# A two-level product kernel on one core: where weight sums, one PSUM add and the next x are placed

## The chip, the cores and the metric

The kernel runs on one core of a Trainium2 chip. The core has five engines that run side by side: TensorE (PE in the profile, its weight loads are PEld), VectorE (DVE), ScalarE (ACT), GpSimd (POOL) and SyncE (SP), which here only issues transfers. The metric is the time of one execution on the device, in microseconds (us), as the median of seven executions.

## The reference

The reference is an attention without softmax, followed by a feed-forward block that multiplies two projections of the same input:

```python
kv = np.einsum('bhsd,bhse->bhde', k, v)          # 8 batches, 8 heads, 576 tokens, 64 per head
out = np.einsum('bhsd,bhde->bhse', q, kv)
rms = np.sqrt(np.mean(out * out, axis=-1, keepdims=True) + 1e-06)
x = out / rms * g_norm                            # then (8,8,576,64) -> (4608, 512)
a = x @ w1                                        # 512 -> 1024
b = x @ w2
h = a * b @ w3                                    # 1024 -> 1024
return h @ w_out                                  # 1024 -> 512
```

All inputs to the kernel's arithmetic are 32-bit floats on the chip; the weights come in 64 bits and are converted first.

## The kernel before, in words

**Start.** The kernel converts the weights and multiplies `w3 @ w_out` into one matrix, `w3o_sb`, so that the feed-forward block becomes `(x@w1 * x@w2) @ w3o`. This ends near 84 us.

**Groups.** The tokens are worked in nine groups of 512. Groups T = 0 to 7 hold the first 512 tokens of one batch each; group T = 8 (called `B` in the code) holds the last 64 tokens of all eight batches. The order is 0 to 6, then 8, then 7 (L976). For every group there are two stages: the gates (`a * b`, kept in `ab`) and the projection (`ab @ w3o`).

**Products in the manner of Strassen and Winograd.** Each large product is cut into 2 x 2 blocks and made with seven products of blocks in place of eight (`winograd`, L611). This needs sums of the blocks of the weights (`sums`: s1, s2, s4, and s3 in the place of a21) and of the moving side (`combine`: t1, t2, t4, and t3 in the place of b12). The results are put together from the products in PSUM and from copies that ACT makes of some of them: p1, p5, u2 and u3. The copies u2 and u3 share one buffer, so u3's copy waits until u2 has been read.

**Gates (L743).** For T = 0 to 6 the gates go through p = 0 to 3, one scheme of seven products for each p; each gives one part of `ab` as four blocks c12, c22, c11, c21 (an add on DVE, L757, and a multiplication, L758; for c21 a copy on ACT and a multiplication, L753 and L754). After each p DVE sums the blocks of `ab` for the projection (`sum_ab`, L730). In the middle of each scheme stands `between`, which is called twice for each p and carries the attention of the next batch in pieces (`steps`, L519): k-v products, the q part, the norm (L378: squares on ACT, reduction L385 on DVE, square root L389 on ACT, reciprocal and multiplication on DVE) and the turning of x and q by copies on POOL (L291, L293, L305) and transposing transfers on SP (L295).

**Projection (`project_twice`, L1016).** From T = 1 on each of its seven block products is itself cut in the same way (two levels). DVE makes the inner sums (`sum_inner`, L1001, written into three rotating places `inner_sums[n % 3]`), PE makes seven times seven small products, ACT copies results from PSUM, and DVE joins them (`add`, L1089, and `finish`, L1066). The weights of this product are prepared once in T = 1, stored in DRAM, and loaded back for each projection (`load_b`, L979). The argument `ahead` is the list of four subtractions on DVE that combine the next group's x (`combine_x`); they were called after `sum_inner(2)`.

**The last two groups (T = 8 and T = 7, `TWICE`).** Their gates for p = 2 are made in the usual way, then those for p = 0 and 1 in two levels (`gates_of_two`, L824), then p = 3 in the usual way. The inner sums of the weights for these (7 sets of s1, s2, s4, called the weights' sums here) are made ahead by `prepare_w` (L770) in T = 3 and T = 4, stored to DRAM by three transfers for each set, and loaded back later (`load_w`). Each set takes three DVE instructions (L775 to L777), which go into one of the three places of `inner_sums`; before the change the sets took turns between the first and the third place.

In `gates_of_two` the products 0 and 2, 4, 6 go through one pair of PSUM banks (r1), 3 and 5 through another (r2), product 1 through a third (r3). p1 and p5, u2, u3 and a last one are copied to SBUF by ACT (`keep`); `add` on DVE adds a product to a copy straight from PSUM; `finish` joins the four parts.

**What sets the order.** PE, POOL and SP run their instructions in the order in which the program is written; so does DVE from p = 3 of a group to the end of its projection, and from `gates_of_two` to the end in the last two groups (`manual_schedule`). The other instructions of DVE, and ACT's, are put in order by a planner when the program is built: it may set an instruction earlier than where it is written, also among those whose order is written out. `tc.issue_after(ins)` keeps the instructions made inside it behind `ins` on the same engine; it says nothing of how far behind. On each engine an instruction that waits holds up all those behind it.

Of the kernel before, what the change touches and what calls it, by code (L numbers as in the profile page):

```python
# [3 lines left out]

# [8 lines left out]
FP32 = mybir.dt.float32  # L13
# [9 lines left out]
def kernel(  # L23
# [32 lines left out]
    nc = tc.nc  # L56
# [551 lines left out]
    def late_tile(name):  # L608
        return late_pool.tile([P, 7, P], FP32, name=name[0] if name[0] == "u" else name)
# [160 lines left out]
    def prepare_w():  # L770

        for n, (name, _) in enumerate(PRODUCTS):
            a11, a12, a21, a22 = w_blocks(name)
            s1, s2, s4 = inner_sums[2 * (n % 2)]
            nc.vector.tensor_add(s1, a21, a22)  # L775
            nc.vector.tensor_sub(s2, s1, a11)
            nc.vector.tensor_sub(s4, a12, s2)  # L777
            for i, s in enumerate((s1, s2, s4)):
                at = (3 * n + i) * 2 * P
                nc.sync.dma_start(  # L780
                    out=w_l2[:, at:at + 2 * P].rearrange("p (w m) -> p w m", w=2), in_=s
                )
            yield
# [40 lines left out]
    def gates_of_two(T):  # L824

        if not places:
            other = work.tile([P, 2, 2, NP // 2, N], FP32, name="xT")
            other = other.rearrange("p i j r n -> p (i j r n)")
            places.extend([other[:, 0:PART // 2], other[:, 1024:1024 + PART // 2]])
            other = work.tile([P, 2, 2, 4, D], FP32, name="xn", bufs=1)  # L830
            places.append(other.rearrange("p i l m d -> p (i l m d)")[:, 0:PART // 2])
            places[:] = [t.rearrange("p (n t) -> p n t", t=P) for t in places]

        def products(n, w, ps, new):
            a_name, b_name = PRODUCTS[n]
            a11, a12, s3, a22 = (t[:, w] for t in w_blocks(a_name))
            s1, s2, s4 = (
                loaded_w[q // 7][:, q % 7 * 2 * P + w * P:q % 7 * 2 * P + (w + 1) * P]
                for q in range(3 * n, 3 * n + 3)
            )  # L840
            b11, _, b21, b22 = (
                xb[T][b_name][:, c, i * P:(i + 1) * P] for c in range(2) for i in range(2)
            )
            t1, t2, t3, t4 = x_sums[n]
            seen = set()
            for place, x, y in (
                (0, a11, b11), (3, a12, b21), (1, a22, t4), (2, s1, t1), (6, s2, t2), (5, s4, b22),
                (4, s3, t3),
            ):
                nc.tensor.matmul(  # L850
                    ps[place // 4][:, place % 4, :], lhsT=x, rhs=y,
                    start=new and place // 4 not in seen, stop=True, skip_group_check=True,
                )
                seen.add(place // 4)
            if w == 1 and n in (2, 4, 6):
                load_b()
            return ps

        def banks(pool, tag):
            return [bank(pool, tag).rearrange("p (i n) -> p i n", n=P) for _ in range(2)]  # L860

        def keep(t, ps):
            nc.scalar.copy(t[:, 0:4], ps[0])
            nc.scalar.copy(t[:, 4:7], ps[1][:, 0:3])
            return t

        def add(z, ps):
            nc.vector.tensor_add(z[:, 0:4], ps[0], z[:, 0:4])
            nc.vector.tensor_add(z[:, 4:7], ps[1][:, 0:3], z[:, 4:7])

        def finish(z, w, i, j):

            def wide(i):
                return z[:, i:i + 1].to_broadcast([P, 2, P])

            dst = ab[i][:, 0:2, j, :].rearrange("p m (n t) -> p m n t", t=P)
            to = dst
            if w:
                to = late_pool.tile([P, 2, N], FP32, name="c").rearrange("p m (n t) -> p m n t", t=P)
            nc.vector.tensor_add(z[:, 6], z[:, 6], z[:, 0])  # L880
            nc.vector.tensor_add(z[:, 4:6], z[:, 4:6], wide(6))
            nc.vector.tensor_add(to[:, 1], z[:, 1:3], wide(4))
            nc.vector.tensor_add(to[:, 0], z[:, 3:6:2], z[:, 0:3:2])
            if w:
                nc.vector.tensor_mul(dst, dst, to)

        for w in range(2):
            r1 = products(0, w, banks(ps_mm, "mm"), True)
            p1 = keep(late_tile("p1"), r1)
            r3 = products(1, w, banks(ps_at, "at"), True)  # L890
            add(p1, r3)
            finish(p1, w, 0, 0)
            products(2, w, r1, False)
            z = keep(late_tile("u2"), r1)
            r2 = products(3, w, banks(ps_mm, "mm"), True)
            p5 = keep(places[2] if w else late_tile("p5"), r2)
            products(4, w, r1, False)
            u3 = keep(places[0], r1)
            nc.vector.tensor_add(p5, p5, u3)
            finish(p5, w, 1, 1)  # L900
            products(5, w, r2, False)
            add(z, r2)
            finish(z, w, 0, 1)
            products(6, w, r1, False)
            finish(keep(places[1], r1), w, 1, 0)
        loaded_w.clear()

    def sum_ab_two():
# [92 lines left out]
    def sum_inner(n, between=lambda: None, place=None):  # L1001

        s1, s2, s4 = ab_sums
        x = [ab[0][:, :, 0], s1, s2, s4, ab[0][:, :, 1], ab[1][:, :, 0], ab[1][:, :, 1]][n]
        a11, a12, a21, a22 = (
            x[:, 2 * j:2 * j + 2, i * P:(i + 1) * P] for i in range(2) for j in range(2)
        )
        s1, s2, s4 = inner_sums[(n if place is None else place) % 3]
        nc.vector.tensor_add(s1, a21, a22)  # L1009
        nc.vector.tensor_sub(s2, s1, a11)  # L1010
        nc.vector.tensor_sub(s4, a12, s2)
        between()
        nc.vector.tensor_sub(a21, a11, a21)  # L1013
        inner[n] = [a11, a12, a22, s1, s2, s4, a21]

    def project_twice(T, last, ahead, load_after):  # L1016
# [97 lines left out]
        p1 = keep("p1", r1)  # L1114
        load_b()
        sum_inner(2)
        for f in ahead:
            f()
        r2 = products(1)
        p5 = keep("p5", r2)  # L1120
        load_b()
# [2 lines left out]
        z = keep("u2", r1)  # L1124
        load_b()
        sum_inner(4)
        products(3, r2)
        if not done[T]:
            load_b()
# [136 lines left out]
    for n, T in enumerate(groups):  # L1266
        pieces = steps(T + 1) if n + 2 < NG else iter([])

        at = count()

        def between():
            next(pieces, lambda: None)()
            if T == 1:
                for _ in range(2):
                    if next(preparing, 0) == 0 and len(loaded_b) < 3:
                        load_b()
            if T in (3, 4) and next(at) in (0, 2, 3, 5):
                next(preparing_w, 0)
            if T == B - 2 and p == 2 and not replaced:
                replaced.append(True)  # L1280
                replace_a21()
# [11 lines left out]
        for p in range(NF):  # L1293
            if T in TWICE and p + 1 < NF:
                continue
            if T and p + 1 == NF:
                sum_1, sum_2, sum_4, sum_3 = sum_ab(p)
                following = {
                    "c12": [], "c22": [sum_1],
                    "c11": [  # L1300
                        lambda: sum_inner(0, lambda: all_of(f() for f in (sum_2, sum_3))),
                        lambda: sum_inner(1),
                    ],
                    "c21": [sum_4],
                }

                if T in TWICE:
                    following["c12"] += of_two[:1]
                    following["c22"] += of_two[1:]
                else:  # L1310
                    in_order = tc.manual_schedule(engines={mybir.EngineType.DVE})
                    in_order.__enter__()
                gates(T, p, between, lambda name: all_of(f() for f in following[name]))
                continue
            gates(T, p, between if T or p else lambda: None)
            if T == 0:
                if p + 1 < NF:
                    run(sum_w(p + 1))
                for n in range(2):
                    if len(converted) < len(todo):  # L1320
                        ahead = [copies["xT"] if p == 0 else copies["u3"][0], copies["u2"][p]][n]
                        with tc.issue_after(ahead.ins):
                            begin_next()
                        end_next()
                if p + 1 == NF:
                    allocate_projection()
                    run(*(f(i) for i in range(NF) for f in (sum_ab, combine_w3o)))
            else:
                run(sum_ab(p))
        last = n + 1 == NG  # L1330
        if T:
            project_twice(
# [40 lines left out]
```

## Time and profile before

| | |
|---|---|
| median of 7 executions | 765.32 us (765.01 to 766.04) |
| profiled execution, its own time | 765.32 us |
| its span, first to last instruction | 763.5 us |
| instructions | 15003 |
| granted TensorE clock, mean | 1.00 |
| transfers | 140.84 MB, mean 184 GB/s |
| stages in the span | start to 84 us; T=0 and 1 to 243; T=2 to 319; T=3 to 395; T=4 to 473; T=5 to 548; T=6 to 623; T=8 to 691; T=7 to the end |

How to read the lines: in the timeline each line gives the start in us from the span's start, the duration, the engine, the line of the kernel, the operation, what it writes and reads (by the program's names, buffer numbers left out), the shape and a count; in brackets stands how long the engine was idle just before and whose work ended that. Tiles cut from one larger buffer carry that buffer's name: `raw` holds, among others, the sums of `ab`, the first place of `inner_sums` and the output blocks; the third place is `inner_sums`; the second lies in the tail of `w3o_sb` and in `raw`. Ends of matmuls are modelled. The chain of work follows the span back from its end, at each step to what released it.

### The profile page before, as it was taken

Reading aid. Unit: us, or ns where it says so; the run is one execution under the profiler, and the core shown is the slowest. Engines: PE = TensorE matmul, PEld = TensorE weight load, DVE = VectorE, ACT = ScalarE, POOL = GpSimd, SP = SyncE. Lnnn points to the kernel's source line nnn. Section 1 sums busy time; section 2 is a strip of 40 time slices with the busy share of each in tenths; the row PEclk is TensorE's granted clock in tenths of the full one; section 3 lists DMA queues with packets and bytes.
Section 4 is the critical chain, followed back from the end, with each engine's and each line's share of the span. In section 5 each row is a group of like instructions: output and inputs, shape, how many; then the busy total and the mean of one; then the engine's idle time right before and its main releaser. Section 6 shows DMA issues by size and latency. Waiting matters only on the chain.

```text
span 763.5 us, 15003 instructions
## 1 busy us (share of the span) xinstructions
PE 755.1 (99%) x5943; PEld 661.0 (87%) x5943; DVE 585.7 (77%) x1167; ACT 263.4 (34%) x499; POOL 165.0 (22%) x190
## 2 busy tenths in 40 slices
PE   8999999999999999999999999999999999999998
PEld 6455788888899889988998899889988999999997
DVE  7978999548878568967786588567867777997797
ACT  6777763213322332232222322332233213322421
POOL 0000000223510442043104320431053125006100
PEclk9999999999999999999999999999999999999999
DMA  9997641338997835694669466835652470466244
GB/s 317 342 334 204 195 146 35 84 84 255 332 297 260 241 98 163 217 242 142 187 209 258 135 166 223 218 95 164 227 128 59 152 220 35 145 204 190 92 138 144
DMA packets 137050, 140.84 MB, mean 184 GB/s; under 512 B 77076, under 2 KB 124308, under 8 KB 136980
## 3 DMA queue, kind: packets, MB, share of 16 engines
q1 hardware_dynamic: 134528, 125.46, 55.0%
q10 hardware_dynamic: 2452, 14.42, 5.6%
q8 instruction: 47, 0.77, 0.4%
q14 instruction: 23, 0.19, 0.1%
HBM read 105.78 MB, written 19.14 MB: 164 GB/s over the span
## 4 chain that ended last, share of the span: by engine, by line
PE 83%; issue 6%; DMA 4%; DVE 3%; POOL 2%; ACT 1%; SPq 1%; POOLq 0%; ACTq 0%
PE mm L618 45%; PE mm L1051 19%; PE mm L597 7%; PE mm L850 5%; PE at L333 2%; PE at L416 2%; DMA raw<-in_moe_w_out_dram 1%; PE at L850 1%; PE at L584 1%; DMA w_l<-raw 1%; DMA xn<-xT 1%; DMA q_sb<-qT 1%; POOL xT L305 1%; POOL qT L305 1%; PE at L352 1%
## 5 line engine op out<-in xcount | busy, mean ns | idle before, releaser
L618 PE MATMUL mm<-xT,w_sb 128*128 128x256 f32 x720 | 165.2, 379 | 0.0
L618 PEld LDWEIGHTS mm<-xT,w_sb 128*128 128x128 f32 x720 | 136.3, 190 | 18.7 <-issue 0.5
L618 PE MATMUL mm<-xc,ws 128*128 128x256 f32 x512 | 116.3, 380 | 0.8 <-ACT p L631 0.8
L618 PEld LDWEIGHTS mm<-xc,ws 128*128 128x128 f32 x512 | 96.9, 190 | 14.9 <-ACT p L631 1.7
L631 ACT COPY u<-mm 128x512 f32<-128x512 f32 x66 | 38.7, 587 | 122.6 <-PE mm L618 114.0
L291 POOL COPY xT<-xn 128x1024 uint16<-128x1024 uint16 x26 | 31.1, 1226 | 179.4 <-DVE xn L394 179.4
L757 DVE TENSOR_TENSOR c<-mm,u 128x512 f32<-128x512 f32 x32 | 22.0, 688 | 59.7 <-PE mm L618 59.7
L631 ACT COPY p<-mm 128x512 f32<-128x512 f32 x66 | 38.5, 585 | 73.7 <-PE mm L618 66.0
L597 PE MATMUL mm<-chunks,ab 128*128 128x512 f32 x128 | 60.3, 603 | 1.7 <-DVE chunks L171 1.4
L618 PE MATMUL mm<-xc,w_sb 128*128 128x256 f32 x256 | 61.4, 383 | 0.0
L618 PE MATMUL mm<-xT,ws 128*128 128x256 f32 x240 | 57.3, 382 | 0.0
L758 DVE TENSOR_TENSOR ab<-c 128x256 f32<-128x256 f32 x96 | 52.7, 549 | 2.5
L618 PEld LDWEIGHTS mm<-xc,w_sb 128*128 128x128 f32 x256 | 47.8, 190 | 6.9 <-ACT u L631 0.3
L385 DVE TENSOR_REDUCE inv<-sq 128x8 f32<-128x512 f32 (+1 forms) x40 | 23.4, 626 | 35.4 <-ACT sq L384 35.4
L618 PEld LDWEIGHTS mm<-xT,ws 128*128 128x128 f32 x240 | 44.9, 190 | 6.2
L1051 PE MATMUL mm<-w3o_sb,ab 128*128 128x128 f32 x368 | 49.1, 276 | 0.2
L1051 PE MATMUL mm<-w3o_sb,raw 128*128 128x128 f32 x372 | 48.6, 276 | 0.0
L1051 PEld LDWEIGHTS mm<-w3o_sb,ab 128*128 128x128 f32 x368 | 45.5, 192 | 1.2 <-DVE ab L1013 0.6
L1051 PEld LDWEIGHTS mm<-w3o_sb,raw 128*128 128x128 f32 x372 | 44.9, 192 | 0.5 <-DVE raw L1009 0.2
L1062 ACT COPY u<-mm 128x512 f32<-128x512 f32 x23 | 13.5, 587 | 85.8 <-DVE raw L1075 57.1
L597 PEld LDWEIGHTS mm<-chunks,ab 128*128 128x128 f32 x128 | 21.8, 190 | 24.2 <-issue 15.8
L305 POOL COPY xT<-xn 128x1024 uint16<-128x1024 uint16 x26 | 30.7, 1208 | 50.9 <-DMA xn<-xT 50.9
(300 smaller groups left out, 1368.2 us busy)
## 6 DMA issues: line engine op xcount, KB each, us to landing
w3o_sb<-w3o_l SPq DMA_DIRECT2D x18, 896.0 KB, 4.8
raw<-in_moe_w_dram SPq DMA_DIRECT2D x31, 512.0 KB, 7.5
raw<-w3o_l SPq DMA_DIRECT2D x15, 896.0 KB, 4.6
w3o_sb<-w3o_l ACTq DMA_DIRECT2D x14, 896.0 KB, 4.5
k_sb<-in_k_dram SPq DMA_DIRECT2D x32, 256.0 KB, 4.2
v_sb<-in_v_dram SPq DMA_DIRECT2D x32, 256.0 KB, 4.7
q_sb<-in_q_dram SPq DMA_DIRECT2D x32, 256.0 KB, 4.7
out_dram<-raw SPq DMA_DIRECT2D x14, 512.0 KB, 3.6
```

Source lines behind the costliest of these rows:

```text
L291: nc.gpsimd.tensor_copy(to, src.rearrange("p a n w -> p w a n"))
L305: nc.gpsimd.tensor_copy(words(dst), src)
L333: nc.tensor.matmul(kv_ps[e * D:(e + 1) * D, r - rs[0], :], lhsT=k_sb[:, e, cols] if j < J else kl[:, 2 * r + e, :], rhs=v_sb[:, e, cols] i ...
L385: nc.vector.tensor_reduce(out=inv[:, i], in_=sq.rearrange("p (h d) -> p h d", d=D), axis=AX.X, op=ALU.add)
L416: nc.tensor.matmul(o_ps[l][tokens, n * D:(n + 1) * D], lhsT=qT[r][rows, e, i, tokens], rhs=kv_b[rows, e, r, :], start=True, stop=True,)
L597: nc.tensor.matmul(sums_ps[half][m], lhsT=w3T[half, c][:, m, :], rhs=chunks[:, c, 1, :], start=(c == 0), stop=(c == KF - 1),)
L618: nc.tensor.matmul(ps[:, u, :], lhsT=lhsT(a_name, u, c), rhs=rhs(b_name, c),  start=(u == 0 and c == 0 and to is None), stop=(c == chunks ...
L631: copies.setdefault(name, []).append(nc.scalar.copy(t, ps))
L757: nc.vector.tensor_add(c, one, two)
L758: nc.vector.tensor_mul(dst, c[:, 0, :], c[:, 1, :])
L850: nc.tensor.matmul(ps[place // 4][:, place % 4, :], lhsT=x, rhs=y, start=new and place // 4 not in seen, stop=True, skip_group_check=True,)
L1051: nc.tensor.matmul(to[:, i, :], lhsT=x[:, c, :], rhs=y[:, c, :], start=new and place // 4 not in seen, stop=(c == 1), skip_group_check=True,)
```

## The change

Three things move, and a few instructions go.

1. **Weights' sums.** They are no longer called inside `between`. In T = 3 and T = 4 they are called after `sum_ab(p)` and tied behind its last instruction: two sets after p = 1 and two after p = 2 in T = 3, two after p = 1 and one after p = 2 in T = 4. They now take turns through all three places of `inner_sums`. Their transfers on SP move with them in the written order.
2. **Third joined product of `gates_of_two`.** The product that was copied as u3 and then added to p5 is added to p5 straight from PSUM by `add`: two ACT copies and one DVE add of 896 elements become two DVE adds of 512 and 384. The buffers `places` shrink from three to two.
3. **Next x.** In `project_twice` the list `ahead` runs after `sum_inner(4)`, no longer after `sum_inner(2)`.

```diff
         for n, (name, _) in enumerate(PRODUCTS):
             a11, a12, a21, a22 = w_blocks(name)
-            s1, s2, s4 = inner_sums[2 * (n % 2)]
+            s1, s2, s4 = inner_sums[n % 3]
...
-            other = work.tile([P, 2, 2, 4, D], FP32, name="xn", bufs=1)
-            places.append(other.rearrange("p i l m d -> p (i l m d)")[:, 0:PART // 2])
...
-            p5 = keep(places[2] if w else late_tile("p5"), r2)
+            p5 = keep(places[1] if w else late_tile("p5"), r2)
             products(4, w, r1, False)
-            u3 = keep(places[0], r1)
-            nc.vector.tensor_add(p5, p5, u3)
+            add(p5, r1)
             finish(p5, w, 1, 1)
             products(5, w, r2, False)
             add(z, r2)
             finish(z, w, 0, 1)
             products(6, w, r1, False)
-            finish(keep(places[1], r1), w, 1, 0)
+            finish(keep(places[0], r1), w, 1, 0)
...
         sum_inner(2)
-        for f in ahead:
-            f()
         r2 = products(1)
...
         sum_inner(4)
+        for f in ahead:
+            f()
         products(3, r2)
...
-        at = count()
-
         def between():
...
-            if T in (3, 4) and next(at) in (0, 2, 3, 5):
-                next(preparing_w, 0)
...
             else:
-                run(sum_ab(p))
+                ops = [step() for step in sum_ab(p)]
+                with tc.issue_after(ops[-1].ins):
+                    for _ in range({(3, 1): 2, (3, 2): 2, (4, 1): 2, (4, 2): 1}.get((T, p), 0)):
+                        next(preparing_w)
```

More of the change, by code (lines that the diff above doesn't have):

```diff
@@ L1 @@
 from contextlib import ExitStack
-from itertools import count, islice
+from itertools import islice
 from types import SimpleNamespace
```

## The prediction

> **What bounds the kernel now.** I read the page first, then PE's pauses in the timeline, then what ended each. Groups of tokens are named by their T. Page, busy time and the chain's shares:
>
> ```profile
> PE 755.1 (99%) x5943; PEld 661.0 (87%) x5943; DVE 585.7 (77%) x1167; ACT 263.4 (34%) x499; POOL 165.0 (22%) x190
> PE 83%; issue 6%; DMA 4%; DVE 3%; POOL 2%; ACT 1%; SPq 1%; POOLq 0%; ACTq 0%
> ```
>
> PE is the bound and the change touches no matmul, so only PE's pauses can be won. In the timeline, weight loads start every 0.216 us in the gates (8 in 1.73) and every 0.112 in the inner products. A later start I count as a pause. From 84 us on, those of 0.15 us or more that are not in every group are: T=1's projection 0.26, 0.30, 0.15 (at 226, 231, 232); start of T=3 0.23 (322); T=4 0.24 (398) and 1.20 (413); T=6 0.29 and 0.25; T=8 0.17 and 0.38 (669, 671); T=7 0.19 and 0.38. Sum 4.0 us: no change of the other engines wins more. Two kinds matter. First, T=4, timeline of weight loads and of DVE and ACT:
>
> ```profile
> 408.24 0.84 DVE L775 TENSOR_TENSOR raw<-w_sb 128x256 f32<-128x256 f32 x1 [0.97 <-DMA w_l<-raw]
> 411.35 0.41 DVE L776 TENSOR_TENSOR raw<-raw,w_sb 128x256 f32<-128x256 f32 x1
> 411.79 0.43 DVE L777 TENSOR_TENSOR raw<-w_sb,raw 128x256 f32<-128x256 f32 x1
> 412.14 1.27 DVE L385 TENSOR_REDUCE inv<-sq 128x8 f32<-128x512 f32 x2
> 413.44 0.31 ACT L389 ACTIVATE inv<-inv,eps_col 128x16 f32<-128x16 f32 x1 [3.03 <-DVE inv L385]
> 413.66 1.05 ACT L631 COPY p<-mm 128x512 f32<-128x512 f32 x2
> 414.27 1.59 PEld L618 LDWEIGHTS mm<-xc,ws 128*128 128x128 f32 x8 [1.23 <-ACT p L631]
> ```
>
> A weight sum (L775) waits 0.97 us for the landing of an earlier sum's transfer; behind it on DVE stand two sums of ab, the other two weight sums and the norm's reduction; ACT stands at the square root that needs the reduction, with p1's copy behind it; and PE needs that copy to reuse the bank. Loads were due at 411.35 + 1.73 = 413.07 and came at 414.27. At the starts of T=3 and T=4 the same sums sit inside the tail of the projection before:
>
> ```profile
> 319.91 0.41 DVE L775 TENSOR_TENSOR raw<-w_sb 128x256 f32<-128x256 f32 x1
> ...
> 321.78 0.41 DVE L1075 TENSOR_TENSOR raw<-p 128x256 f32<-128x256 f32 x1
> ...
> 322.29 0.59 ACT L631 COPY p<-mm 128x512 f32<-128x512 f32 x1 [2.16 <-DVE raw L1075]
> 322.92 1.16 PEld L618 LDWEIGHTS mm<-xc,ws 128*128 128x128 f32 x6 [0.26 <-ACT p L631]
> ```
>
> The second kind is DVE as the chain itself, in T=8 (T=7 alike):
>
> ```profile
> 665.48 0.59 ACT L631 COPY u<-mm 128x512 f32<-128x512 f32 x1 [2.87 <-PE mm L618]
> 666.14 0.68 DVE L757 TENSOR_TENSOR c<-p,u 128x512 f32<-128x512 f32 x1
> 667.67 0.69 DVE L915 TENSOR_TENSOR raw<-ab,raw 128x512 f32<-128x512 f32 x1
> 671.85 0.52 PEld L1051 LDWEIGHTS mm<-w3o_sb,ab 128*128 128x128 f32 x4 [0.30 <-DVE ab L1013]
> ```
>
> **The change, part by part. A: the weights' sums.** The edge behind the last sum of ab keeps the seven sets (21 DVE sums of some 0.42 us, 21 transfers on SP) out of the projections' tails and out of T=4's first half. It moves them; none goes.
> What is taken away: in each tail six sums at a pitch of 0.33 to 0.45 us, 2.0 to 2.7 us; p1's copy then waits for PE alone, and the 0.23 and 0.24 go whole. In T=4 the wait (0.97), the first sum (0.76 until the next starts at 409.00) and the other two (0.79) leave the reduction 2.5 us earlier, 409.6 in place of 412.1. The square root then ends by 411.2, before p1's product is ready (first loads 411.35 + 0.2), and 1.20 goes whole. Were only the wait taken away, 0.97 of it would go. T=5 and T=6, which have no weight sums, start with no pause. Gain 0.23 + 0.24 + 1.20 = 1.67.
> What is added: two sets behind p = 1 in T=3 (from 348.6) and T=4 (from 424.6), two behind p = 2 in T=3 (from 365.0), one in T=4 (from 444.2). Alone, a set takes 3 x 0.45; beside POOL's copies single sums took 1.14 to 1.26 (at 333.7 and 350.3). Two sets are thus 2.0 to 4.5 us. The cover is DVE's idle time there, rows of DVE's timeline in T=3:
>
> ```profile
> 354.79 1.28 DVE L385 TENSOR_REDUCE inv<-sq 128x8 f32<-128x512 f32 x2 [2.79 <-ACT sq L384]
> ...
> 364.54 0.43 DVE L672 TENSOR_TENSOR raw<-ab,raw 128x256 f32<-128x256 f32 x1
> 368.22 0.69 DVE L757 TENSOR_TENSOR c<-mm,u 128x512 f32<-128x512 f32 x1 [3.25 <-PE mm L618]
> ...
> 373.20 0.42 DVE L1009 TENSOR_TENSOR raw<-ab 128x256 f32<-128x256 f32 x1
> ```
>
> After p = 1 there are 6.1 us in T=3 (348.6 to 354.8) and 6.8 in T=4 (the reduction at 431.45 waited 6.81): covered. After p = 2 in T=4 1.5 us for 1.35: covered. After p = 2 in T=3 3.25 us for 2.0 to 4.5, with POOL copying from 365.46 to 367.71: two sums at 1.2 and four at 0.45 are 4.2, so L757 starts about 0.9 late. Behind it, u3's copy (369.88 in the trace, after PE) needs L757 done: 368.22 + 0.9 + 0.69 = 369.8, just in time. If that cover is short, the projection's sums behind it start late, and they have only 0.15 us to spare (L1013 ends 375.55, PE loads its result at 375.70). Bounds of this cost: 0, and 4.5 - 3.25 = 1.3. I take 0.0, since 0.9 lies inside the slack.
> The transfers: SP is kept at the six DMAs until their sums are done, near 353.5, and the loads of k and v that followed at 352.35 come 1.2 us later; pair for pair they are read by PE in the next group, tens of us on. Cost 0. At 369 nothing follows on SP but L993 at 371.60, which waits for PE. The fourth set now uses the first buffer, which the projection's first sum (373.20) overwrites: its transfer, issued about 368.7, lands 1.8 to 2.0 us later in the quiet rows (347.80, 366.59), at 370.7; with the worst row (6.08, at 402.13) at 374.8, a wait of 1.6. I take the quiet rows, since SP's neighbours there are the same; 0, other end 1.6.
>
> **B: p5 + u3 straight from PSUM** (four times). ACT loses two copies (0.59 and 0.48), DVE's add of 896 elements (pitch 1.13, 654.28 to 655.41) becomes two from PSUM (pitch 0.60 + 0.58 = 1.18, L1090 and L1091 at 243.02 and 243.62). They start when the copy started (653.10), not at 654.28, so DVE's chain runs 1.1 us ahead. PE's seventh product in that bank must now wait for DVE: adds end at 654.3, loads are due at 654.97, 0.65 to spare (643.3 against 644.03 for w = 0). Where does the 1.1 go? DVE reaches c12's add at 663.8 (u2's copy at 662.03 + 1.74, as in T=3), not 664.48, and then c22's add, which needs u3's copy: 665.48 + 0.59 = 666.07, on PE's clock. It starts at 666.10 in place of 666.14. What is late next is ACT's copy, and L915's 0.6 behind it still stands. So 0.04 in each of T=8 and T=7, 0.08. Bounds: 0, and all of both groups' pauses, 1.12.
> At this place a rule speaks against the change: the Trainium skill, "Perfetto Trace Analysis", section "Optimizing Scalar/DVE Operations", puts a DVE instruction's access at about 60 ns on SBUF and 125 ns on PSUM, so two PSUM reads for one SBUF read are an estimated 0.19 us more DVE time each, 0.76 over four. By the rows above it is 0.05 each, 0.2 over four; by either the sum keeps its sign.
>
> **C: next x combined later.** Its four subtractions (0.79 + 0.61 + 0.60 + 0.60 = 2.6 us) pass behind sums 3 and 4, and all of it still ends where the add of u2 begins (385.50 in T=3), so DVE's later work does not move; SP, POOL and ACT have nothing in the step. Sums 3 and 4 come 2.6 us earlier. That takes away T=1's 0.30 and 0.15, where sum 3 ran at 231.27 while PE was at its product. But in T=1 DVE is busy without idle time to p1's last sum (245.33 to 245.75), and T=2's p1 copy waits for it (1.97 <-DVE raw L1075) and ends at 246.42; PE needed it at 243.07 + 3.35 = 246.42. PE arrives 0.45 earlier and waits 0.45 there. Gain 0, bounds 0 and 0.45.
>
> **Sum.** 1.67 + 0.08 + 0 = 1.75 us. The profiled execution took 765.32 us, a span of 763.5 and 1.8 around it, and equals the median of the seven runs, so 765.32 - 1.75 = 763.6 us. About 0.2%, 1.53 us, is what can be told from no change: below 763.8 counts as faster, above 766.85 as slower.
>
> **Rivals.**
> 1. T=3's second place has too little cover: DVE's lateness or the buffer's landing reaches the projection, 0.7 to 1.6 us are given back, 764.3 to 765.2. For it: 4.2 us of sums in 3.25 of idle time. Against: the quiet landings and u3's slack.
> 2. T=4's long pause is POOL's, not the sums': two sums of ab took 1.25 beside POOL's copy at 407.76 (rows L672). If the reduction stays behind them, half of 1.20 remains: 764.2 to 764.7. Against: the reduction could then start at 410.6 and still be in time.
> 3. Better: DVE's lead in B or C reaches PE, up to 1.04 and 0.45 more, 762.1 to 763.1. Against: u3's copy and p1's wait.
> 4. Slower: the edge sets only the earliest place of the sums, not the latest. If the order made for DVE puts the three sets of p = 2 into the projections, which have 0.15 us to spare, each costs 3 x 0.45 = 1.35 us of PE: 4.05, and 763.6 + 4.05 = 767.6. It decides from 1.75 + 1.53 = 3.3 us, that is from all three sets on; one set only eats most of the gain. For it: before, the sums did land inside projections. Against: DVE's idle time stands right behind the edge.
>
> **How the numbers follow.** Main case 0.56, 763.2 to 764.1, of which 0.46 below 763.8; rival 1 0.16; rival 2 0.10; rival 3 0.09; rival 4 0.09. Faster 0.46 + 0.09 = 0.55; same 0.10 + 0.16 + 0.10 = 0.36; slower 0.09. The range leaves out rival 4 and the better half of rival 3, and ends with rival 1: 762.7 to 765.3.
>
> **What would show it.** A right: no L775 between L1072 rows; p1's copies near 321.3 waiting for PE; no pause at 413; L775 to L777 in T=3 only after L672 at 348 and 365. Wrong: L1009 at 373 waiting for DMA, or a PE load near 375.7 released by L1013. B right: c12's add earlier, c22's add still right after ACT's u copy, PE's 0.3 pause at 671.85 still there. C right: no pause at 231, a new one near 246 released by ACT p. The prediction falls if T=4's pause stays, or if one of DVE's leads is handed on to PE.

## The result, and the profile after

The changed kernel takes 764.2 us (median; 763.4 to 765.4). The kernel before, run on the same chips, took 765.7 us (764.7 to 769.3). The ratio is 0.9977, with a 95% interval of 0.9969 to 0.9984: 1.2 to 2.4 us less, 1.8 in the middle (0.0023 x 765.7), where the prediction had taken off 1.75; the two medians differ by 1.5. That lies just about at what can be told from no change.

Lines of code behind L830 stand two or three numbers lower in the changed kernel (L1009 is now L1006, L1013 is L1010, L1051 is L1048, L1072 to L1075 are L1069 to L1072, L915 is L912). The page of the changed kernel, busy time and the chain's shares:

```profile
PE 755.4 (99%) x5943; PEld 662.0 (87%) x5943; DVE 591.7 (78%) x1171; ACT 259.5 (34%) x491; POOL 165.9 (22%) x190
PE 96%; DMA 2%; DVE 2%; ACT 1%; issue 0%; SPq 0%; ACTq 0%
```

PE does the same work; DVE is busy 6 us longer, and the chain of work now runs through PE for 96% in place of 83%. These shares are no measure of the gain: before, the chain leaves PE at T = 4's long pause (414.27) and follows DVE, POOL and transfers back to about 332 us. The profiled execution's span is 762.4 us, against 763.5. It started 0.35 us later at the first gates (83.91 against 83.56), so its times are 0.35 higher there, and lower only behind the place of T = 4's long pause.

What counts are PE's pauses. I took the pitch of PE's weight loads in each trace, and counted by how much a pitch exceeds the usual one of its kind, from 0.12 us up and from 215 us on, leaving out one pause of 0.14 at about 277 and one at about 430 that every run has. The table, in us, for the changed kernel, the one before and every experiment told below:

| kernel | T=1 and start of T=2 | starts of T=3 and T=4, and T=4 at 413 | T=3's projection | T=6 | T=8 and T=7 |
|---|---|---|---|---|---|
| before | 0.71 | 0.23 + 0.24 + 1.20 | 0 | 0.54 | 1.13 |
| changed | 0.79 | 0 | 0 | 0.54 | 1.02 |
| changed, another execution | 0.42 | 0 | 0 | 0.54 | 1.02 |
| sums tied alone | 0.71 | 0 | 0 | 0.54 | 1.11 |
| edge, two places | 0.72 | 0 | 0 | 0.54 | 1.12 |
| three places alone | 0.67 | 0.87 + 0.86 + 0 | 0 | 0.54 | 1.09 |
| PSUM add alone | 1.53 | 0.22 + 0.23 + 1.20 | 0 | 0.54 | 1.02 |
| next x alone | 0.63 | 0.24 + 0.23 + 1.20 | 0 | 0.54 | 1.10 |
| one set in a projection | 1.53 | 0 | 1.01 | 0.54 | 1.01 |
| s4 later | 1.33 | 0 | 0 | 0.54 | 0 |
| places swapped | 0.52 | 0 | 0 | 0.54 | 1.02 |
| places swapped, next x early | 1.14 | 0 | 0 | 0.54 | 1.02 |
| s4 later, places swapped | 1.71 | 0 | 0 | 0.54 | 0 |
| s4 later, no PSUM add | 2.55 | 0 | 0 | 0.54 | 0 |

In the gates such a pause counts 0.11 us too much. The first load after it is followed by the next one 0.108 us later, not 0.216, so half a pitch is made up at once. It can be read from the lines: the eight loads ahead of T = 4's long pause in the kernel before span 1.70 us, the eight behind it (the line at 414.27 in the prediction) only 1.59.

```profile
411.35 1.70 PEld L618 LDWEIGHTS mm<-xc,ws 128*128 128x128 f32 x8
```

All kernels here make the same 5943 loads in the same order of shapes, so the n-th load of one trace can be laid beside the n-th of another. Between before and changed, the shift of the loads steps by 0.124 and 0.128 at the starts of T = 3 and T = 4 and by 1.09 at 413: 1.34 us, where the table has 1.67. At 246 the changed kernel loses 0.24, where the pitch shows 0.35. Among the small products of the projections the two ways differ by 0.01 a pause.

The second column holds, besides what the change does, a wait for a transfer that differs from execution to execution; it is told in the last section. The third column is where most of the time went.

T = 4 of the changed kernel, timeline of DVE, ACT and the weight loads, in the place of the long pause:

```profile
408.81 1.28 DVE L385 TENSOR_REDUCE inv<-sq 128x8 f32<-128x512 f32 x2 [0.69 <-ACT sq L384]
410.36 0.31 ACT L389 ACTIVATE inv<-inv,eps_col 128x16 f32<-128x16 f32 x1
411.40 1.70 PEld L618 LDWEIGHTS mm<-xc,ws 128*128 128x128 f32 x8
411.82 0.59 ACT L631 COPY p<-mm 128x512 f32<-128x512 f32 x1 [1.15 <-PE mm L618]
```

The norm's reduction no longer stands behind weights' sums: it waits for ACT's squares, 3.3 us earlier than before. The square root is through before p1's product is ready, p1's copy waits for PE, and PE goes on without a pause.

The new places of the sums in T = 3, timeline of DVE, POOL and ACT, first behind p = 1, then behind p = 2:

```profile
347.50 0.42 DVE L775 TENSOR_TENSOR raw<-w_sb 128x256 f32<-128x256 f32 x1
...
348.50 0.42 DVE L672 TENSOR_TENSOR raw<-ab,raw 128x256 f32<-128x256 f32 x1
348.84 1.38 DVE L777 TENSOR_TENSOR raw<-w_sb,raw 128x256 f32<-128x256 f32 x1
...
354.97 1.28 DVE L385 TENSOR_REDUCE inv<-sq 128x8 f32<-128x512 f32 x2 [2.55 <-ACT sq L384]
...
365.66 2.68 POOL L305 COPY xT<-xn 128x1024 uint16<-128x1024 uint16 x2 [1.91 <-DMA xn<-xT]
365.96 1.37 DVE L777 TENSOR_TENSOR inner_sums<-ws,inner_sums 128x256 f32<-128x256 f32 x1
...
367.25 1.37 DVE L776 TENSOR_TENSOR raw<-raw,ws 128x256 f32<-128x256 f32 x1
...
369.00 0.68 DVE L757 TENSOR_TENSOR c<-mm,u 128x512 f32<-128x512 f32 x1
...
370.06 0.59 ACT L631 COPY u<-mm 128x512 f32<-128x512 f32 x1 [2.81 <-PE mm L618]
...
373.39 0.43 DVE L1006 TENSOR_TENSOR raw<-ab 128x256 f32<-128x256 f32 x1
...
375.88 0.53 PEld L1048 LDWEIGHTS mm<-w3o_sb,ab 128*128 128x128 f32 x4
```

Behind p = 1 DVE still has 2.55 us of idle time before the reduction. Behind p = 2 two sums beside POOL's copies took 1.37 each, and c12's add (L757) follows with no idle time before it; but u3's copy waits for PE, not for that add, L1006 waits for no transfer, and PE's loads at 375.88 wait for nobody. The cover held.

The start of T = 2, timeline, which is where the earlier sums of part C are given back:

```profile
245.69 0.42 DVE L1072 TENSOR_TENSOR raw<-p 128x256 f32<-128x256 f32 x1
...
246.20 1.29 ACT L631 COPY p<-mm 128x512 f32<-128x512 f32 x2 [2.27 <-DVE raw L1072]
...
246.84 1.16 PEld L618 LDWEIGHTS mm<-xc,ws 128*128 128x128 f32 x6 [0.37 <-ACT p L631]
```

ACT's copy of T = 2's first product waits for the last sum of p1 on DVE, and PE's loads wait for the copy.

T = 8, timeline: the new PSUM pair of the second half (L866 and L867, and what follows on DVE), then the stretch from c22's add to the pause that stayed:

```profile
652.09 0.69 DVE L866 TENSOR_TENSOR xT<-mm,xT 128x512 f32<-128x512 f32 x1 [0.67 <-PE mm L848]
...
652.75 0.56 DVE L867 TENSOR_TENSOR xT<-mm,xT 128x384 f32<-128x384 f32 x1
...
653.35 0.29 DVE L878 TENSOR_TENSOR xT<-xT 128x128 f32<-128x128 f32 x1
...
664.45 0.59 ACT L631 COPY u<-mm 128x512 f32<-128x512 f32 x1 [2.87 <-PE mm L618]
665.07 0.69 DVE L757 TENSOR_TENSOR c<-p,u 128x512 f32<-128x512 f32 x1 [0.52 <-ACT u L631]
...
666.59 0.68 DVE L912 TENSOR_TENSOR raw<-ab,raw 128x512 f32<-128x512 f32 x1
...
670.77 0.52 PEld L1048 LDWEIGHTS mm<-w3o_sb,ab 128*128 128x128 f32 x4 [0.30 <-DVE ab L1010]
```

DVE is ahead and idles 0.52 us for u3's copy, which is on PE's clock. From there the same sums follow as before, L912 among them, and PE waits the same 0.38 (0.30 of it by the line's own idle time) for L1010.

### The profile page after: what moved, and what is told of

The parts are those of the page before. It is cut to its first block, busy times and chain, and to the rows that moved or that the text cites. A ratio compares the mean times of both kernels' runs of the same rounds, so it can differ in the third digit from the quotient of the medians.

```text
span 762.4 us, 15002 instructions
## 1 busy us (share of the span) xinstructions
PE 755.4 (99%) x5943; PEld 662.0 (87%) x5943; DVE 591.7 (78%) x1171; ACT 259.5 (34%) x491; POOL 165.9 (22%) x190
## 4 chain that ended last, share of the span: by engine, by line
PE 96%; DMA 2%; DVE 2%; ACT 1%; issue 0%; SPq 0%; ACTq 0%
PE mm L618 53%; PE mm L1048 22%; PE mm L597 7%; PE mm L848 5%; PE at L333 3%; PE at L416 2%; DMA raw<-in_moe_w_out_dram 1%; PE at L848 1%; PE at L584 1%; PE at L352 1%; PE at L1099 0%; DMA raw<-in_moe_w_dram 0%; PE at L450 0%; DVE c L757 0%; DVE ab L758 0%; PE at L435 0%
## 5 line engine op out<-in xcount | busy, mean ns | idle before, releaser
L757 DVE TENSOR_TENSOR c<-mm,u 128x512 f32<-128x512 f32 x32 | 22.0, 688 | 61.2 <-PE mm L618 61.2
L758 DVE TENSOR_TENSOR ab<-c 128x256 f32<-128x256 f32 x96 | 55.6, 579 | 2.5
L1048 PE MATMUL mm<-w3o_sb,ab 128*128 128x128 f32 x368 | 49.1, 276 | 0.2
L1048 PE MATMUL mm<-w3o_sb,raw 128*128 128x128 f32 x372 | 48.2, 275 | 0.0
L1048 PEld LDWEIGHTS mm<-w3o_sb,ab 128*128 128x128 f32 x368 | 45.5, 192 | 1.2 <-DVE ab L1010 0.6
L1048 PEld LDWEIGHTS mm<-w3o_sb,raw 128*128 128x128 f32 x372 | 44.7, 192 | 0.2 <-DVE raw L1008 0.2
L305 POOL COPY xT<-xn 128x1024 uint16<-128x1024 uint16 x26 | 31.7, 1246 | 50.9 <-DMA xn<-xT 50.9
```

Source lines behind the costliest of these rows:

```text
L305: nc.gpsimd.tensor_copy(words(dst), src)
L757: nc.vector.tensor_add(c, one, two)
L758: nc.vector.tensor_mul(dst, c[:, 0, :], c[:, 1, :])
L1048: nc.tensor.matmul(to[:, i, :], lhsT=x[:, c, :], rhs=y[:, c, :], start=new and place // 4 not in seen, stop=(c == 1), skip_group_check=True,)
```

## The experiments

Each ratio is that to the kernel before, measured beside it, with its 95% interval.

**Part A alone.** The kernel before with the edge and the third place:

```diff
-            s1, s2, s4 = inner_sums[2 * (n % 2)]
+            s1, s2, s4 = inner_sums[n % 3]
...
-            if T in (3, 4) and next(at) in (0, 2, 3, 5):
-                next(preparing_w, 0)
...
-                run(sum_ab(p))
+                ops = [step() for step in sum_ab(p)]
+                with tc.issue_after(ops[-1].ins):
+                    for _ in range({(3, 1): 2, (3, 2): 2, (4, 1): 2, (4, 2): 1}.get((T, p), 0)):
+                        next(preparing_w)
```

> The kernel before with part A alone: weights' sums tied behind the sums of ab, three places used in turn. My theory (A makes nearly all of the gain): the pauses of 0.23 (start of T=3), 0.24 (start of T=4) and 1.20 (T=4, at 413) are gone, T=1's 0.30 and 0.15 and the 0.38 of T=8 and T=7 stay; 1.67 us less, ratio 0.9978. Rival (the parts need each other, DVE's lead in the last two groups is worth something): less than 1.3 us, ratio above 0.9983.

Measured: 764.27 us, ratio 0.9983 (0.9974 to 0.9991). All three pauses of the third column are gone, and no new one came in T = 3 or T = 4. The profiled execution had 0.41 more at 191, where PE waited behind a copy of ACT that waited for DVE; no other trace shows it. Part A is 1.3 us of the ratio by itself. Its pauses are 1.67 us by the pitch and 1.34 by loads laid side by side. The ratio stands on the line that was drawn for the rival, so the time does not decide between the two; the pauses do, since parts B and C take away no more than 0.1 us each in what follows.

**Part B alone.** The kernel before with u3's product added from PSUM:

```diff
             products(4, w, r1, False)
-            u3 = keep(places[0], r1)
-            nc.vector.tensor_add(p5, p5, u3)
+            add(p5, r1)
             finish(p5, w, 1, 1)
```

> The kernel before with part B alone: the third joined product of the two-level gates added from PSUM. My theory: DVE runs about 1 us ahead in T=8 and T=7 and the lead ends at u3's copy on ACT; PE's pauses of 0.38 stay within 0.05, time less by 0.1 us or less, ratio 0.9999. Rival (DVE was the chain there, so its lead counts): both pauses go, 1.1 us less, ratio 0.9986. Other rival (PE waits for DVE to free the bank): a new pause of PE inside the two-level gates, slower.

Measured: 765.47 us, ratio 0.9996 (0.9987 to 1.0004). In T = 8 and T = 7 the first pause went from 0.17 and 0.19 to 0.13 each, the second stayed at 0.38. That is 0.1 us, as in the changed kernel, and below what the time can tell.

**Part C alone.** The kernel before with `ahead` moved:

```diff
         sum_inner(2)
-        for f in ahead:
-            f()
...
         sum_inner(4)
+        for f in ahead:
+            f()
```

> The kernel before with part C alone: next x combined two inner sums later. My theory: T=1's pauses of 0.30 and 0.15 go and one of about 0.45 comes at the start of T=2, released by ACT's copy of p1; time the same, ratio 1.0000. Rival (the 0.45 is won): 0.45 us less, ratio 0.9994.

Measured: 765.48 us, ratio 0.9992 (0.9983 to 1.0001). The pauses at 231 and 232 are gone; 0.15 at 239.9 and 0.34 at 246.4 came. T = 1 and the start of T = 2 together have 0.63 in place of 0.71. By loads laid side by side the steps are 0.46 won and 0.15 and 0.23 lost: the move trades waits of nearly the same size, 0.08 us apart.

**The third place alone.** Is T = 4's pause made by the wait for the transfer or by the sums that stand there? The kernel before with one line changed:

```diff
-            s1, s2, s4 = inner_sums[2 * (n % 2)]
+            s1, s2, s4 = inner_sums[n % 3]
```

> The kernel before, with only the places of the weights' sums changed to three in turn; where the sums are called stays as before. My theory (wait for a landing and queue behind it make T=4's pause): the 0.97 us wait for the transfer goes, the pause at 413 falls from 1.20 to about 0.2, those at the starts of T=3 and T=4 stay at 0.23 and 0.24; 1.0 us less, ratio 0.9987. Rival (POOL's copies beside DVE make the pause): the pause stays above 0.6, ratio above 0.9992. If the whole 1.20 goes, the two sums behind cost nothing.

Measured: 766.26 us, ratio 1.0003 (0.9994 to 1.0012). The 1.20 is gone, and still nothing is won: the pauses at the starts of T = 3 and T = 4 grew from 0.23 and 0.24 to 0.87 and 0.86. The start of T = 3, timeline of this kernel:

```profile
318.15 0.42 DVE L775 TENSOR_TENSOR inner_sums<-ws 128x256 f32<-128x256 f32 x1
...
321.43 0.41 DVE L775 TENSOR_TENSOR raw<-w_sb 128x256 f32<-128x256 f32 x1
...
323.30 0.41 DVE L1075 TENSOR_TENSOR raw<-p 128x256 f32<-128x256 f32 x1
...
323.81 1.07 ACT L631 COPY p<-mm 128x512 f32<-128x512 f32 x2 [2.79 <-DVE raw L1075]
...
324.44 0.73 PEld L618 LDWEIGHTS mm<-xc,ws 128*128 128x128 f32 x4 [0.89 <-ACT p L631]
```

Three sets (L775 at 313.67, 318.15 and 321.43) now stand in the tail of T = 2's projection, before the L1075 on which p1's copy waits; before there were two (316.63 and 319.91), and it is the same at the start of T = 4. The places are all that was edited, so it was the turn of two places that had kept the third set out; that the planner hoists it because no transfer has to be waited for is the likely reason. By loads laid side by side 1.26 us came in the two tails and 1.09 went in T = 4. All expectations that left the sums where they were in the tails fall with it.

**The edge alone, with two places.** Part A without the line of the experiment above:

```diff
-            if T in (3, 4) and next(at) in (0, 2, 3, 5):
-                next(preparing_w, 0)
...
-                run(sum_ab(p))
+                ops = [step() for step in sum_ab(p)]
+                with tc.issue_after(ops[-1].ins):
+                    for _ in range({(3, 1): 2, (3, 2): 2, (4, 1): 2, (4, 2): 1}.get((T, p), 0)):
+                        next(preparing_w)
```

> The kernel before with the weights' sums tied behind the sums of ab, but the two places in turn as before. My theory (the edge alone makes A's gain, the third place none): pauses at 322, 398 and 413 gone, no sum waits for a landing; 1.67 us less, ratio 0.9978. Rival (the third place is needed at the new place too): a sum waits for a transfer of the set two before, and some of the gain is missing.

Measured: 764.09 us, ratio 0.9978 (0.9969 to 0.9987). The three pauses are gone here too, 1.34 us by loads laid side by side as in part A alone. The whole gain of part A is the edge's; the third place adds nothing measurable beside it.

**One set in a projection.** How much does the slower rival cost for each set? The changed kernel with the two sets of T = 3's p = 2 taken away, one of them put on DVE right before the projection's first inner sums, the other moved to T = 4:

```diff
                 else:
+                    if T == 3:
+                        following["c11"].insert(0, lambda: next(preparing_w))
                     in_order = tc.manual_schedule(engines={mybir.EngineType.DVE})
...
-                    for _ in range({(3, 1): 2, (3, 2): 2, (4, 1): 2, (4, 2): 1}.get((T, p), 0)):
+                    for _ in range({(3, 1): 2, (4, 1): 3, (4, 2): 1}.get((T, p), 0)):
```

> The changed kernel with one set of weights' sums of T=3 put on DVE just before the projection's first inner sum (two sets after p=1 in T=3, three and one in T=4, so that seven are made). My theory (the fourth rival's price: 0.15 us to spare there): PE pauses 1.2 us near 376, 1.35 for the set less 0.15; 1.2 us more than the changed kernel, ratio to the kernel before 0.9993. Rival (the pause is made up later, or there is more to spare): less than 0.5 us more.

Measured: 765.57 us, ratio 1.0004 (0.9995 to 1.0014). The timeline of T = 3's projection in this kernel:

```profile
373.85 0.42 DVE L775 TENSOR_TENSOR inner_sums<-ws 128x256 f32<-128x256 f32 x1
...
375.58 1.44 PEld L1048 LDWEIGHTS mm<-w3o_sb,raw 128*128 128x128 f32 x12 [0.37 <-DVE raw L1006]
...
377.50 0.52 PEld L1048 LDWEIGHTS mm<-w3o_sb,ab 128*128 128x128 f32 x4 [0.48 <-DVE ab L1010]
```

PE waits twice for inner sums that stand behind the set, 0.45 and 0.56 us by the pitch of its loads, 1.01 in all. The gain in time is gone; 1.01 is more than half of it, and the rest of the difference is of the size of T = 1's varying wait (1.53 here, 0.79 in the changed kernel), so only the 1.01 is shown.

**Is L915 (now L912) the cause of the pause that stays in T = 8 and T = 7?** The changed kernel with the inner sum s4 of the first half called one result later:

```diff
                     following["c12"] += of_two[:1]
-                    following["c22"] += of_two[1:]
+                    following["c21"] += of_two[1:]
```

> The changed kernel with the two-level gates' s4 (L912, 0.6 us on DVE) called after c21 in place of after c22. My theory (what keeps DVE's lead from PE in the last two groups is u3's copy and, behind it, this one sum): PE's pauses in T=8 and T=7 (0.135 + 0.376 each) go, 1.0 us less than the changed kernel, ratio to the kernel before 0.9964. Rival (the chain behind c22 is late anyway, or s4 is missed at its new place): pauses stay or come back further on, ratio 0.9977.

Measured: 763.5 us, ratio 0.9973 (0.9964 to 0.9982). The timeline of T = 8 in this kernel:

```profile
667.82 0.68 DVE L757 TENSOR_TENSOR c<-mm,p 128x512 f32<-128x512 f32 x1
...
670.93 0.41 DVE L1010 TENSOR_TENSOR ab<-ab 128x256 f32<-128x256 f32 x1
...
671.50 0.53 PEld L1048 LDWEIGHTS mm<-w3o_sb,ab 128*128 128x128 f32 x4
...
673.64 0.68 DVE L912 TENSOR_TENSOR raw<-ab,raw 128x512 f32<-128x512 f32 x1
```

L912 now runs at 673.64, behind the sums that PE needs; L1010 ends 0.16 us before PE loads its result, and all four pauses of the two groups are gone, 1.02 us. So what bounded PE there was one instruction of DVE in a place where DVE is the chain, and not the copy that part B took away.

**Does part B have a share in that?** The kernel before with part A, part C and the later s4, u3 still copied by ACT (the diff to the kernel before is those of part A and part C above, and the one just shown):

> s4 after c21, with parts A and C but without part B (u3 of the two-level gates is copied by ACT and added from SBUF as before). My theory (u3's copy of the gates of p=3 sets DVE's pace whichever way, so B's lead is worth nothing here too): pauses in T=8 and T=7 stay away or are at most 0.05 each; same time as with B within 0.1 us. Rival (with s4 gone from the chain DVE's lead from B is what keeps PE going): pauses of 0.3 or more in T=8 and T=7, 0.6 us more than with B.

Measured: 763.15 us, ratio 0.9965 (0.9951 to 0.9979). The pauses of T = 8 and T = 7 are gone without part B as well. From this kernel's timeline of T = 8:

```profile
665.46 0.59 ACT L631 COPY u<-mm 128x512 f32<-128x512 f32 x1 [2.87 <-PE mm L618]
...
666.12 0.69 DVE L757 TENSOR_TENSOR c<-p,u 128x512 f32<-128x512 f32 x1
```

c22's add stands right behind u3's copy here too, with no idle time of DVE before it: without part B, DVE is later and still in time. Whether the times agree within 0.1 us, as expected, cannot be told from them (763.15 and 763.5).

**Is part C's lost gain the wait for p1's buffer?** The changed kernel with the buffers of p1 and p5 in the projection exchanged, so that the next group's first copy does not go into the one that is read last:

```diff
-        p1 = keep("p1", r1)
+        p1 = keep("p5", r1)
...
-        p5 = keep("p5", r2)
+        p5 = keep("p1", r2)
```

> The changed kernel with the places of the projection's p1 and p5 exchanged, so that the next gates' first copy waits for p5's end, some 2.7 us earlier, and no longer for p1's. My theory (C's 0.45 was lost at T=2's copy of p1): the pause of 0.35 at 246 goes and those at 231 stay away; 0.3 us less than the changed kernel, ratio to the kernel before 0.9973. Rival (DVE's lateness reaches PE at the next copy anyway): a pause of the same size one product later, ratio 0.9977.

Measured: 764.19 us, ratio 0.9985 (0.9977 to 0.9994). The timeline of this kernel at the start of T = 2:

```profile
244.80 0.59 ACT L631 COPY p<-mm 128x512 f32<-128x512 f32 x1 [1.25 <-PE mm L618]
...
245.02 0.42 DVE L1072 TENSOR_TENSOR raw<-p 128x256 f32<-128x256 f32 x1
```

The copy now waits for PE and starts before DVE's last sum of p1 (245.02) has begun: the exchange takes the wait for p1's buffer away, and in the changed kernel's lines above it is this wait that ends just before PE's. The 0.35 at 246 is gone, the 0.155 at 239.75 too, but that the exchange did it is not shown. T = 1 waited 0.52 us for a transfer in this execution, and DVE caught up meanwhile: against the changed kernel its last sum of p1 comes 0.67 us earlier (245.02 against 245.69), PE's loads before it only 0.38 (244.38 against 244.76). Kernels without the exchange whose T = 1 waited longer, s4 later (1.33) and no PSUM add (2.55), have neither of the two pauses; from the latter's timeline:

```profile
246.43 0.59 ACT L631 COPY p<-mm 128x512 f32<-128x512 f32 x1 [1.25 <-PE mm L618]
```

An estimate from this kernel's lines: a copy that had waited for the sum, which ends at 245.44, would have ended about 0.7 later, at 246.1, and PE's ninth load was due at 244.38 + 8 x 0.216 = 246.1, so hardly any pause would have been left. In the time nothing can be seen; what was to be won is less than the interval can tell.

**And with the next x early again,** the kernel above with `ahead` back after `sum_inner(2)`:

```diff
         sum_inner(2)
+        for f in ahead:
+            f()
...
         sum_inner(4)
-        for f in ahead:
-            f()
```

> The same exchange, with next x combined early again, as before the change. My theory: T=1's pauses of 0.30 and 0.15 come back, nothing at 246; 0.3 to 0.45 us more than with x combined late. Rival (C is worth nothing wherever p1 stands): the same time as with x combined late.

Measured: 764.46 us, ratio 0.9984 (0.9975 to 0.9992). The pauses at 231 and 232 are back (0.56 and 0.15), nothing stands at 246. T = 1 waited for a transfer here too (0.42). That part C, freed of the wait for p1's buffer, is worth what it takes away in T = 1, a few tenths of a us, is argued and not shown: the medians' 0.27 is too little for it.

**Both together,** the changed kernel with the later s4 and the exchanged buffers (the two diffs above):

> The changed kernel with both additions: s4 of the two-level gates after c21, and the projection's places of p1 and p5 exchanged. My theory: the 1.02 us of pauses in T=8 and T=7 and the 0.35 at 246 go; 1.0 to 1.4 us less than the changed kernel, ratio to the kernel before 0.9962. Rival (the exchange is worth nothing, since T=1 waits for a late transfer instead): 1.0 less, ratio 0.9966.

Measured: 763.32 us, ratio 0.9969 (0.9959 to 0.9980). From T = 2 on only T = 6's 0.54 us and the two small pauses that every run has are left. T = 1 waited 1.71 us in this execution, so it says no more than the kernel above of what the exchange is worth.

**The changed kernel once more,** with no edit, beside the last ones:

> The changed kernel once more, beside the others of this set. Expected: as measured, ratio 0.9977; pauses in T=8 and T=7 0.135 and 0.376, at 246 about 0.35; the pauses of T=1's projection differ from run to run with the landing of its transfers.

Measured: 764.28 us, ratio 0.9978 (0.9969 to 0.9987). The kernels with a later s4 stand 0.8 to 1.1 us below it, as their pauses say (1.02). The intervals of the ratios overlap, so in the times alone this is likely rather than shown; the pauses show it.

## Why the prediction was right

The sum was 1.75 us and the ratio says 1.8 (1.2 to 2.4), the medians 1.5. The time that was forecast, 763.6, started from 765.32; from the 765.7 of the kernel before as it ran here it would be 764.0, and 764.2 was measured, inside the range. That the kernel is faster by more than 0.2%, which was held most likely, is not shown. In the two traces the pauses by the pitch differ by 1.70 (4.05 - 2.35), but loads laid side by side come only 1.49 us closer to the start of the gates. So the waits named are the right ones, while the closeness of 1.75 to 1.8 is in part luck: the largest term was read 0.33 too high, and the interval holds both. Point by point:

- **What bounds the kernel.** Right: DVE's busy time grew by 6 us and the time fell.
- **A, the gain of 1.67.** Right in place and cause: all three pauses are gone, and the edge alone takes them away. Mis-sized: PE gets 0.124 + 0.128 + 1.09 = 1.34 us for them. The reading took the late start of one load for the loss, and each of the three makes up 0.108 with the next load. The reduction came 3.3 us earlier, not 2.5: the two sums of `ab` (L672) that had taken 1.25 beside POOL's copy had both begun (407.36 and 407.70) before that copy did (407.82) and took 0.43 and 0.42. So rival 2 fell, whose price rested on their 1.25.
- **A, the aside "Were only the wait taken away, 0.97 of it would go".** Wrong. The third place alone took the wait away and the whole pause went in T = 4, but 1.26 came in the two tails ((0.87 + 0.86) - (0.23 + 0.24)), and the time did not fall. The step that failed is that the other sums stay where they are: the order came out anew with the edit. The edge alone made the gain.
- **A, the new places.** The cover behind p = 1 held. The sums began 1 us earlier than taken, at 347.50, since the edge is tied to the last sum of `ab` in the written order (s3, L672 at 347.16), and on DVE another one (348.50) comes after it. Behind p = 2 the two slow sums cost 2 x 0.95 more than the others, as the 4.2 us had it; c12's add came 0.60 us late against PE (369.00 - 368.22, less 0.18 by which PE itself is later there), not 0.9, and u3's copy still waited for PE. The transfer of the fourth set landed in time. Cost 0, so rival 1 fell. The loads of k came 0.57 us later, not 1.2, and nobody waited for them.
- **B, 0.08.** Measured 0.10 in pauses, in three traces. In the clock of before, c12's add came at 663.8 (662.79 and 1.03 by which this stage is earlier), and c22's add 0.03 behind the end of u3's copy, as worked out. The lead ended there in 0.52 us of idle time. One term was mis-sized: the pair from PSUM took 0.66 + 0.60 = 1.26 in place of 1.18, so it costs 0.13 more than the add it replaces, not 0.05. The row I took was of a pair that came straight behind other work of DVE; this one had waited for PE. The Trainium skill's "Perfetto Trace Analysis", section "Optimizing Scalar/DVE Operations", had given an estimated 0.19; the measurement lies between and hides behind the idle time either way.
- **C, 0.** Right within 0.1: 0.30 + 0.15 went, 0.35 + 0.155 came, or 0.46 against 0.39 by loads laid side by side. The prediction had put all of it at 246, as 0.45; 0.155 of it stands at 239.75. At 246 the lines show p1's buffer as the wait: the copy waits for the last sum of p1, and PE for the copy.
- **Rival 3.** Fell in this kernel: neither lead reached PE. The 1.0 that it priced for T = 8 and T = 7 can be had by one more edit, the later s4, for which part B's lead is not even needed. Whether the exchanged buffers give the rest stays open.
- **Rival 4.** Did not come about: no set landed inside a projection. It priced a set at 1.35 and did not take off the 0.15 to spare, which leaves 1.2; the set put there cost 1.01.
- **Not foreseen.** T = 1's pauses were taken as fixed. They vary by up to 2 us between executions (last section). In the two profiles compared they happen to be nearly equal, 0.71 and 0.79, which is luck; between two other single traces they would have hidden the whole effect.

## What to carry to other kernels

Where one engine is busy 99% of the time, add up its pauses, find for each the instruction that ended it, and ask what that instruction stood behind: here one engine's order of instructions, not its load, held most of what was won. Measure a pause by what the engine's later work gains, not by one late start, since part of it can be made up at once. An edge that keeps work out of a stretch is a different thing from taking away the wait inside it, because a planner may set other work into the freed stretch, as the third place alone showed. A lead on an engine can end in a wait before it reaches the path: part B's was worth 0.1 us, and moving one instruction that stood behind that wait was worth 1.0 without it.

## What the runs showed of the hardware that was not expected

**A weight stream in T = 1 that lands late.** The load of `w3o_sb` that SP issues there was issued between 226.5 and 228.0 in every run and took between 4.65 and 8.39 us to land. Up to 5.83 us (before 5.03, changed 5.26) PE did not wait for it; from 6.05 us up PE waited for it, 0.2 to 1.55 us, but for the kernel with one set in a projection. In that one and in the one without the PSUM add PE waited, 1.5 and 1.8 us, for the load that ACT issued 3 us earlier (7.2 and 7.4 us to land there, 4.4 to 5.8 in the others). The chain of work of the kernel with s4 later, from 222 to 237 (start, duration, what), and of the one without the PSUM add:

```profile
221.89 6.04 PE mm L1048 x54
227.94 0.02 issue
227.95 7.18 DMA w3o_sb<-w3o_l
235.13 0.14 issue
235.27 1.80 PE mm L1048 x14
```

```profile
226.53 8.39 DMA w3o_sb<-w3o_l
234.91 0.14 issue
```

The same stretch by windows, from 212 to 235, for the kernel with s4 later and for the one before (the last two columns are the DMA engines' mean share and GB/s):

```profile
212.00:235.00 23.00, 22.18 (x157) 20.83 (x155) 17.68 (x38) 5.33 (x10) 2.44 (x2) 1.00 1.06 296
```

```profile
212.00:235.00 23.00, 22.97 (x164) 21.50 (x163) 17.87 (x38) 5.33 (x10) 2.44 (x2) 1.00 0.96 290
```

The DMA engines are full there in both (mean share 1.06 and 0.96). In every run in which the load took 5.8 us or more, the transposing transfer of q ahead of it on SP was issued late, 2.4 to 3.5 us before the load, and took 6.2 to 8.3 us; in the others it was issued 4.8 to 5.4 us before and took 2.8 to 2.9. That they go together is seen in all runs; what makes the transposes late in some executions is not, and no kernel was made to tell. For the reading of small effects it means that two single executions can differ by up to 2 us in this one place (0.42 and 2.55, in two kernels whose difference lies in T = 8 and T = 7).

**Sums of two SBUF tiles beside POOL's copies** took 1.37 to 1.38 us in place of 0.42, one for each copy of 1.2 to 1.35 us (L777 and L776 beside L305 at 365.66). The Trainium skill's "Perfetto Trace Analysis", section "Optimizing Scalar/DVE Operations", states that GpSimd and VectorE share a read port of SBUF; these rows agree. No experiment moved the copies away.
